# Keys, queries and values placed separately in the load order of an attention + MLP kernel, with a new list of nudges and the last stores in halves

## Chip, cores and metric

One core of one Trainium2 chip. The metric is the device time of that core in microseconds (us), lower is better.

## The reference

```python
def _attn_ref(q, k, v):                       # each (8, 8, 576, 64) fp32
    window = 128
    scores = scale * np.matmul(q, k.transpose(0, 1, 3, 2))
    bias = slopes[:, None, None] * (-np.abs(rel))[None, :, :]
    mask = (rel >= 0) & (rel < window)
    scores = np.where(mask, scores + bias[None], -1000000000.0)
    attn = softmax(scores)                    # cut
    return np.matmul(attn, v)

x = attn_out.transpose(0, 2, 1, 3).reshape(4608, 512)
h = x @ w_in                                  # 512 -> 2048
r = np.maximum(h, 0.0)
return (r * r) @ w_out                        # 2048 -> 512
```

A query looks at itself and the 127 rows before it, so a block of 128 queries needs two blocks of keys. The MLP needs all heads of a row, so a group of 512 rows of `x` can start once its four blocks of attention are done.

## The kernel before

The kernel builds a list of tasks (a load, a burst of matmuls, an exponential, ...) with dependencies, ring buffers, durations and a priority key. A planner in Python works through them with these assumed durations and fixes one order for each engine. On the chip every engine then works in its order, waiting for whatever is late. So keys, slacks and the list of nudges `ADJ` change only orders, never the work.

```python
FIRST = ["b0", "b1", "b2", "b3", "i0", "i1", "i2", "o0", "i3", "i4", "o1", "o2", "b4", "o3", "b5", "b6", "b7"]
N_PE = 8
SLACK = {"kq": 0.0, "kqT": 5000.0, "v": 4000.0, "x": 2000.0}
FILL = 0.7
LEAD = 480
SIZE = {"kq": 4, "v": 9, "kqT": 7, "P": 3, "x": 6}
```

`b` is a block (first 128 rows of one batch) with its keys, queries and values, `i` a piece of `w_in`, `o` a piece of `w_out`. All of these are cast from fp32 to bf16 by DMAs issued on GpSimd, in the planned order; only k0 and q0 come over other queues.

```python
    def load_block(m, key):
        # ... cut: block 0 comes unconverted over the other queues
            def fetch_kq():
                for i, src in enumerate((k, q)):
                    nc.gpsimd.dma_start(view(kq[s_kq[m].idx], i), source(src, m, split))
        # ...
        def fetch_v():
            nc.gpsimd.dma_start(tile_of(s_v[m])[0:n, :, 0:D], source(v, m))
        l_v = plan.add({"POOL": 890.0}, key + 0.2, fetch_v, ...)

    for i, what in enumerate(FIRST):
        n = int(what[1:])
        key = EARLY + 100 * (i + 1)
        if what[0] == "b":
            load_block(n, key)
        else:
            load_w("in" if what[0] == "i" else "out", n, key)
```

Blocks 0 to 7 are transposed on TensorE (`tp` for keys and queries, `xp` for the attention's output), blocks 8 to 39 by DMA transposes on SyncE's queue (`kqT<-kq`, `xT<-x`), which also issues the stores, all in one order.

```python
        if m >= N_PE:
            def flip_x():
                nc.sync.dma_start_transpose(out=xT[:, :, t0:t0 + n], in_=xt[sx.idx][0:n, :])
            t_x[m] = [plan.add({"SP": 1200.0}, due, flip_x, t_n, [], [sx], dma=900.0 * n / 128, name=f"x{m}",
                               slack=SLACK["x"])] * 2
            return
```

Where the planner sees a hole in TensorE's work it places "fillers", useless matmuls on a tile of zeros:

```python
    def fill(task, slot):
        for _ in range(int(task.gap * FILL / 56.0) if task.gap > 200.0 else 0):
            nc.tensor.matmul(slot.tile[:, 0:128], warm[:, 0:128], warm[:, 0:128], start=True, stop=True)
```

Names below: `s` are scores, `P` their exponentials, `pv` the products with the values, `h` the first MLP product, `rt` its relu, `g` the square, `o` the second product. "Group 3" is the fourth group of 512 rows, the first whose four blocks (13 to 16) are all transposed by DMA and used in one go.

The softmax here doesn't subtract the row's maximum and nothing guards it: scores larger than these inputs give would overflow.

## Time and profile before

| | before |
|---|---|
| median of 3 executions | 313.81 us (313.56 to 314.08) |
| span of the profiled one | 311.8 us |
| TensorE starts useful work | 4.58 us |
| lost on TensorE from 4.58 to 25 us | 7.30 us |
| lost on TensorE from 25 us to its end | 8.63 us |
| TensorE ends | 308.78 us |
| tail after it | 3.00 us |

"Lost" is elapsed time less the useful matmuls at their unhindered start-to-start price. The prediction has 7.5 and 8.3 for the two losses; the figures here come from counting useful weight loads (each matmul has one). The profiled execution, at 313.56 us, was the fastest of the three. The prediction shows the lines behind this table. These are three lines of the timelines of ScalarE and TensorE of the kernel before (start, length, engine, line, operation, out<-in, shapes, count, and the idle time before it with what ended it):

```profile
18.73 1.51 ACT L337 ACTIVATE masks<-dist 128x128 bf16<-128x128 f32 x7
20.15 1.05 ACT L762 ACTIVATE rt<-h 128x512 bf16<-128x512 f32 x2
20.77 2.84 PE L798 MATMUL h<-xT,w_in_sb 128*128 128x128 bf16 x48 [0.41 <-ACT rt L762]
```

TensorE stops until 20.77 for a bank of `h`, because the relu that frees the bank stands on ScalarE behind seven mask tiles that nobody needs yet.

### The profile page before, as it was taken

To read this page: it belongs to the slowest core of one execution; us is meant where nothing else is said; L and a number is where in the kernel's file an instruction comes from. 1 tells how busy PE (TensorE), PEld (TensorE's weight loads), DVE (VectorE), ACT (ScalarE), POOL (GpSimd) and SP (SyncE) were. 2 spreads that over 40 slices of the span, in tenths; PEclk is the share of its full clock that TensorE was granted. 3 is DMA by queue.
4 is the path that set the end of the run, shared out by engine and by line. 5 is a ranking of instruction groups with operands and counts; after the bars stand their busy time and mean duration, and the time that the engine had idled before them with its cause. 6 is when DMAs were issued, how large, how long until landed. Compare 5 with 4: busy or idle time off the path is not lost.

```text
span 311.8 us, 7044 instructions
## 1 busy us (share of the span) xinstructions
PE 304.3 (98%) x2767; PEld 173.3 (56%) x2767; DVE 165.5 (53%) x493; ACT 170.9 (55%) x327; POOL 106.4 (34%) x132
## 2 busy tenths in 40 slices
PE   7789999999999999999999999999999999999996
PEld 3588757774676664455555455555444444444443
DVE  5574275675586776687577657776222222222211
ACT  3785456493476376876678737764443444444400
POOL 8953595386622828206747091000000000000000
PEclk9999999999999999999999999999999999999999
DMA  9999999999999999969999999612011100010022
GB/s 129 167 205 206 173 196 176 151 207 161 187 189 176 155 154 203 173 83 139 157 200 182 160 178 151 159 35 69 34 36 57 44 36 35 35 34 36 34 96 72
DMA packets 166242, 39.52 MB, mean 127 GB/s; under 512 B 156353, under 2 KB 161729, under 8 KB 166209
## 3 DMA queue, kind: packets, MB, share of 16 engines
q0 software_dynamic: 115184, 18.10, 83.7%
q1 hardware_dynamic: 50592, 20.65, 33.1%
q8 instruction: 21, 0.34, 0.4%
q10 hardware_dynamic: 432, 0.33, 0.4%
q14 instruction: 13, 0.10, 0.1%
HBM read 36.70 MB, written 9.44 MB: 148 GB/s over the span
## 4 chain that ended last, share of the span: by engine, by line
PE 95%; ACT 2%; DVE 1%; issue 0%; ACTq 0%
PE o L842 40%; PE h L815 27%; PE h L798 13%; PE pv L668 6%; PE s L564 5%; PE wm L475 1%; PE tp L505 1%; ACT P L633 1%; PE s L616 1%; ACT masks L337 1%; ACT kqf L299 1%; PE xp L714 0%; DVE kqf L297 0%; PE s L625 0%; ACT rt L762 0%
## 5 line engine op out<-in xcount | busy, mean ns | idle before, releaser
L842 PE MATMUL o<-w_out_sb,g 128*128 128x512 bf16 (+2 forms) x592 | 142.6, 373 | 0.0
L762 ACT ACTIVATE rt<-h 128x512 bf16<-128x512 f32 (+1 forms) x145 | 86.1, 602 | 95.0 <-PE h L815 70.2
L771 DVE TENSOR_TENSOR g<-rt 128x512 bf16<-128x512 bf16 (+1 forms) x145 | 60.8, 420 | 100.5 <-ACT rt L762 99.4
L815 PE MATMUL h<-xT,w_in_sb 128*128 128x512 bf16 x384 | 97.1, 379 | 0.0
L842 PEld LDWEIGHTS <-g 128*128 128x128 bf16 x592 | 54.1, 98 | 57.0
L588 ACT ACTIVATE P<-s 128x512 bf16<-128x512 f32 x120 | 62.1, 609 | 8.0 <-PE s L564 8.0
L815 PEld LDWEIGHTS <-w_in_sb 128*128 128x128 bf16 x384 | 35.5, 98 | 40.1
L448 POOL DMA_DIRECT2D kq<-in_k_dram x39 | 33.7, 863 | 43.6 <-DMA kqT<-kq 38.0
L798 PE MATMUL h<-xT,w_in_sb 128*128 128x128 bf16 (+1 forms) x512 | 46.0, 246 | 0.4 <-ACT rt L762 0.4
L596 DVE TENSOR_TENSOR P<-P,masks 128x512 bf16<-128x512 bf16 x96 | 39.1, 418 | 8.5 <-ACT P L588 5.3
L798 PEld LDWEIGHTS <-w_in_sb 128*128 128x128 bf16 x512 | 39.0, 98 | 5.5 <-issue 0.5
L453 POOL DMA_DIRECT2D vt<-in_v_dram x32 | 27.3, 854 | 27.9 <-PE pv L668 27.5
L448 POOL DMA_DIRECT2D kq<-in_q_dram x39 | 33.8, 866 | 6.0 <-DMA w_out_sb<-in_moe_w_out_dram 1.8
L694 DVE TENSOR_TENSOR x<-pv,rec 128x256 bf16<-128x256 f32 (+1 forms) x80 | 32.1, 417 | 0.9
L668 PEld LDWEIGHTS <-P 128*128 128x128 bf16 (+1 forms) x576 | 24.2, 101 | 11.9 <-DVE x L694 1.3
L299 ACT ACTIVATE osb<-o 128x512 f32<-128x512 f32 (+1 forms) x23 | 13.4, 583 | 21.2 <-PE o L842 21.2
L668 PE MATMUL pv<-vt,P 128*128 128x65 bf16 (+1 forms) x448 | 22.9, 194 | 0.0
L297 DVE COPY osb<-o 128x512 f32<-128x512 f32 (+1 forms) x14 | 9.5, 681 | 14.7 <-PE o L842 14.4
L564 PEld LDWEIGHTS <-kqT 64*128 64x128 bf16 x448 | 12.4, 94 | 7.6 <-issue 7.0
L685 DVE RECIPROCAL rec<-pv 128x4 f32<-128x4 f32 (+1 forms) x80 | 12.6, 171 | 6.7 <-PE pv L668 5.7
L564 PE MATMUL s<-kqT 64*128 64x128 bf16 (+1 forms) x256 | 15.6, 210 | 0.0
L564 PE MATMUL s<-kqT,kqT 64*128 64x128 bf16 (+1 forms) x192 | 11.4, 210 | 0.0
(45 smaller groups left out, 100.5 us busy)
## 6 DMA issues: line engine op xcount, KB each, us to landing
out_dram<-osb SPq DMA_DIRECT2D x31, 256.0 KB, 5.0
kq<-in_k_dram POOLq DMA_DIRECT2D x31, 128.0 KB, 6.5
kq<-in_q_dram POOLq DMA_DIRECT2D x31, 128.0 KB, 6.8
vt<-in_v_dram POOLq DMA_DIRECT2D x24, 128.0 KB, 6.8
w_out_sb<-in_moe_w_out_dram POOLq DMA_DIRECT2D x4, 512.0 KB, 15.2
w_in_sb<-in_moe_w_in_dram POOLq DMA_DIRECT2D x3, 512.0 KB, 11.5
vf<-in_v_dram POOLq DMA_DIRECT2D x8, 128.0 KB, 6.3
out_dram<-osb SPq DMA_DIRECT2D x8, 128.0 KB, 2.4
```

The source lines that it names most:

```text
L448: nc.gpsimd.dma_start(view(kq[s_kq[m].idx], i), source(src, m, split))
L453: nc.gpsimd.dma_start(tile_of(s_v[m])[0:n, :, 0:D], source(v, m))
L564: nc.tensor.matmul(sS[2 * g2 + r].tile[:, jj * 256 + c0:jj * 256 + c0 + w], tile_of(s_kqT[mk])[rows, c, :], tile_of(s_kqT[mq])[rows, C + c ...
L588: nc.scalar.activation(flat(Pt[sP.idx]), sS[i].tile.rearrange("p (j t) -> p j t", j=2)[:, :, lo:hi], AF.Exp, bias=0.0, scale=scale)
L596: nc.vector.tensor_tensor(flat(Pt[sP.idx]), flat(Pt[sP.idx]), flat(masks), op=ALU.mult)
L668: nc.tensor.matmul(sv.tile[0:n, hi * (D + 1):(hi + 1) * (D + 1)], prob, tile_of(s_v[mk])[:, h, 0:D + 1], start=mk == parts[0][1], stop=mk ...
L694: nc.vector.tensor_tensor(o, heads(sv)[0:n, :, 0:D], sr.tile[0:n, :].unsqueeze(2).to_broadcast([n, 4, D]), op=ALU.mult)
L762: nc.scalar.activation(srt.tile[:, 0:n], slot.tile[:, 0:n], AF.Relu, bias=0.0, scale=1.0)
L771: nc.vector.tensor_tensor(o, i, i, op=ALU.mult)
L798: nc.tensor.matmul(slot.tile[:, f * w:(f + 1) * w], w_in_sb[:, cc, fc * 128:(fc + 1) * 128], xT[:, cc, lo:lo + w], start=cc == 0, stop=cc ...
L815: nc.tensor.matmul(slot.tile, w_in_sb[:, cc, fc * 128:(fc + 1) * 128], xT[:, cc, g * 512:(g + 1) * 512], start=cc == 0, stop=cc == C - 1)
L842: nc.tensor.matmul(slot.tile[:, 0:hi - lo], gt[:, fc, t * 128:(t + 1) * 128], w_out_sb[:, fc, lo:hi], start=fc == 0, stop=fc == FCB - 1)
```

## The change

Its intent: new orders found by replaying the plan with random late landings. Keys/queries (`k`) and values (`v`) of a block get places of their own in the load order; the first piece of `w_in` comes third; the first piece of `w_out` comes before the third of `w_in`; blocks 4 to 7 come last. The last stores before the final one go out in halves. Slacks, the lead of attention, the planner's tie-breaking and all nudges are new.

```diff
-FIRST = ["b0", "b1", "b2", "b3", "i0", "i1", "i2", "o0", "i3", "i4", "o1", "o2", "b4", "o3", "b5", "b6", "b7"]
+FIRST = ["k0", "k1", "i0", "v0", "v1", "k2", "v2", "k3", "v3", "i1", "o0", "i2", "i3", "i4", "o1", "o2", "o3", "k4", "k5", "v4", "k6", "k7", "v5", "v6", "v7"]
+N_XP = 8
+HALVED = [(7, 1), (7, 2), (7, 3)]
-SLACK = {"kq": 0.0, "kqT": 5000.0, "v": 4000.0, "x": 2000.0}
+SLACK = {"kq": 0.0, "kqT": 4500.0, "v": 2000.0, "x": 2500.0}
-LEAD = 480
+LEAD = 1200
 ADJ = {
-    "e12.3": -99552.96, "e17.1": 266.08, ...          # cut: 64 nudges out
+    "b3": 8899994.7, "e13.1": 299208.63, ...          # cut: 59 others in
-    NEAR = {"PE": 60, "ACT": 120, "DVE": 60}
+    NEAR = {"PE": 25, "ACT": 250, "DVE": 0}
-                for t in c:
+                for t in c[:8] if e == "POOL" else c:
-    def load_block(m, key):
+    def load_block(m, key, v_key=None):
-        l_v = plan.add({"POOL": 890.0}, key + 0.2, fetch_v, ...
+        l_v = plan.add({"POOL": 890.0}, key + 0.2 if v_key is None else v_key, fetch_v, ...
-        if m >= N_PE:
+        if m >= N_XP:
         def store():
-            for i, (b, kb) in enumerate(ranges[4 * g + t]):
+            rows = [(b * S + kb * 128, i * 64, blk[kb]) for i, (b, kb) in enumerate(ranges[4 * g + t])]
+            if (g, t) in HALVED:
+                rows = [(r + 64 * i, 64 * i, 64) for r, _, _ in rows for i in range(2)]
```

Cut: the staging buffer of block 0 becomes a ring with one user, and candidates are kept sorted by key. Line numbers after the change are 8 higher in most of the body.

## The prediction

> **What bounds the kernel now.** I read the page first, then busy time by stretches, then the groups of TensorE by shape, the chain of waits over the first 25 us, the timeline of the start and the landing times of the loads. The page says TensorE, nearly alone:
>
> ```profile
> PE 304.3 (98%) x2767; PEld 173.3 (56%) x2767; DVE 165.5 (53%) x493; ACT 170.9 (55%) x327; POOL 106.4 (34%) x132
> PE   7789999999999999999999999999999999999996
> PE 95%; ACT 2%; DVE 1%; issue 0%; ACTq 0%
> ```
>
> Only the first three slices (7.8 us each) and the last are not full. Busy time over four stretches (start, middle, pure MLP, tail):
>
> ```profile
> 4.58:25.00 20.42, 17.09 (x236) 13.16 (x235) 12.34 (x55) 13.19 (x37) 15.18 (x19) 1.00 1.74 185
> 25.00:216.00 191.00, 191.00 (x2082) 116.14 (x2081) 128.03 (x376) 120.98 (x228) 87.40 (x105) 1.00 1.66 162
> 216.00:308.78 92.78, 92.78 (x446) 42.87 (x444) 22.16 (x50) 34.63 (x58) 0.00 (x0) 1.00 0.13 45
> 308.78:311.80 3.02, 0.00 (x1) 0.00 (x0) 0.00 (x0) 0.28 (x1) 0.00 (x0) 1.00 0.25 87
> ```
>
> Columns: length, then busy us (instructions) of PE, weight loads, DVE, ACT, POOL, then clock, DMA share, GB/s. From 25 us until 308.78 TensorE never idles. But a busy PE need not be at its peak, so I took the start-to-start times of the matmuls. In the pure MLP stretch a matmul of 512 columns starts every 216 ns, which is 512 columns at 2.4 per ns plus 2.5 ns; groups of eight of 128 columns come 55.8 ns apart. Pricing every matmul so (two of 64 rows side by side count as one) gives this account of the 311.8 us:
> - 0 to 4.58: warm-up, first load and cast. 4.58 is the first useful matmul.
> - 288.3 us of useful matmuls.
> - 8.3 us lost between 25 and 308.78. Of that 6.4 us are the 30 bursts of 64-row score matmuls, which cost about 119 ns on leaving and 95 ns on entering (30 x 0.214); the rest is mostly the switches to and from pv, 7 to 20 ns each. No stall over 150 ns.
> - 7.5 us lost between 4.58 and 25 (3.3 idle, 0.9 filler matmuls on the zero tile, the rest pipe gaps); useful work done by 16 us is only 5.35, by 22 us 10.0.
> - 3.0 us tail after the last matmul.
>
> So a different order can win only in the start (7.5 us) and a little in the tail. The start hangs on loads. The timeline of GpSimd shows them issued early, then waiting:
>
> ```profile
> 1.34 1.03 POOL L453 DMA_DIRECT2D vf<-in_v_dram  x1 [0.16 <-issue]
> 2.36 0.89 POOL L448 DMA_DIRECT2D kq<-in_k_dram  x1
> ...
> 10.37 2.29 POOL L394 DMA_DIRECT2D w_in_sb<-in_moe_w_in_dram  x3
> 12.58 0.82 POOL L397 DMA_DIRECT2D w_out_sb<-in_moe_w_out_dram  x1
> ...
> 20.00 0.87 POOL L453 DMA_DIRECT2D vf<-in_v_dram  x1 [1.66 <-DMA w_in_sb<-in_moe_w_in_dram]
> 22.52 0.75 POOL L397 DMA_DIRECT2D w_out_sb<-in_moe_w_out_dram  x1 [1.65 <-DMA w_out_sb<-in_moe_w_out_dram]
> ```
>
> The landings in the trace come one after another, in the order of issue: v0 6.24, k1 7.08, q1 7.92, v1 8.77, k2 9.64, q2 10.48, v2 11.32, k3 12.16, q3 13.08, v3 13.88, i0 15.18, i1 16.52, i2 19.70, o0 22.23, i3 24.78, i4 27.36, o1 29.87, o2 32.41, q4 34.15, v4 34.98, o3 37.73, q5 39.48, v5 40.30, and so on to v7 46.85 (k, q, v: block numbers; i, o: pieces of w_in and w_out). A block tile costs 0.85 us of this stream, a 256 KB weight piece 1.3, a 512 KB piece 2.55. The queue is one saturated pipe up to about 45 us. TensorE's stalls in the start sit between these landings:
>
> ```profile
> L625 PE MATMUL s<-kqf 64*128 64x128 bf16 x32 | 2.2, 218 | 1.3 <-DVE kqf L297 0.9
> L668 PE MATMUL pv<-vf,P 128*128 128x65 bf16 x32 | 1.9, 193 | 0.7 <-ACT P L633 0.7
> L278 PE MATMUL tp<-warm 128*128 128x128 bf16 x12 | 0.9, 222 | 0.0
> ```
>
> They are named after the evacuation and the exponential, the links of one block's chain; they show because no other block and no MLP work is there to fill them. The MLP's first matmul starts at 16.01, one us after i0.
>
> **What the Trainium skill says.** "DMA: Bandwidth & Descriptors", section "Issuing engines are not separate DMA queues": all issuers share the same 16 engines and interleave. The trace agrees: DMA is at 9 tenths in nearly every slice up to slice 26, so the order of the list, not the number of queues, decides when a piece lands. "TensorE: Matmul & The Clock Gate", section "Back-to-back issue gap", gives N/2.4 + 2.5 ns as the warm isolated gap and about 131 ns as the sustained figure at N=512. The trace has 216 ns in 220 back-to-back w_out matmuls, so the first form holds here and the second does not; there is no headroom in the MLP. "TensorEngine Tiling (Array Packing)", section "Key Properties": changing the tiling mode drains the engine; here 95 to 119 ns a switch, 6.4 us in all, and the change keeps the number of score bursts. "Perfetto Trace Analysis", section "Identifying the Most-Contended Engine", warns that matmul busy share is no measure of headroom; hence the account by start-to-start times.
>
> **The change part by part.**
> 1. *Load order.* New: k1 q1, i0, v0, v1, k2 q2, v2, k3 q3, v3, i1, o0, i2, i3, i4, o1, o2, o3, k4 q4, k5 q5, v4, k6 q6, k7 q7, v5, v6, v7. The same bytes, so v7 again lands near 46.9. With the durations above, from the same first landing (6.24): q1 7.1 (0.8 earlier), i0 8.4 (6.8 earlier), v0 9.25, v1 10.1, q2 11.8, v2 12.65, q3 14.35, v3 15.2 (1.3 later), i1 16.5 (same), o0 19.1 (3.1 earlier), i2 21.6 (1.9 later), i3 24.2, i4 26.7, o1 29.2, o2 31.8, o3 34.3 (3.4 earlier), q5 37.8, v4 38.6, v5 43 (2.7 later). v0 at 9.25 is no loss: the first exponentials end at 9.26.
>  Working TensorE through this: block 1's transposes and scores come some 1.2 us earlier; x0 is transposed near 11.3 and the first MLP unit (0.45 us) runs in a gap, since i0 is there. By 16.5 the four blocks (about 1.56 us of useful matmuls each, less the last block's pv and transpose) and that unit make about 6.25 us, against 5.7 before. From 16.5 on TensorE should not stall: 2.7 us of units, pv and transposes, 0.9 for the fourth block's unit, then at 19.1 two token tiles of o with the first w_out piece (2 x 0.86, limited by two o banks), which reaches 21.9, past i2 at 21.6. Useful by 21.9: 11.6 us, against 9.9 before. **Gain 1.7 us**, carried to the end because everything later is full. The filler matmuls cost nothing but what waiting would.
> 2. *After 25 us.* i2 to i4 bring 3.57 us of matmuls each per 2.55 us of stream, so no stall to 34; group 0's down projection lasts to about 44.7, and blocks 4 to 7 (keys earlier, v5 later) make about 5 us in between, just enough for v5 at 43. Gain or loss 0.
> 3. *LEAD 480 to 1200*, slacks v 4.0 to 2.0, kqT 5.0 to 4.5, x 2.0 to 2.5, other tie-breaking, a new list of nudges. Attention of blocks 8 to 39 is asked for earlier. It cannot remove work; TensorE was full anyway: 0. It moves attention's end, now at 214 us (last pv), to the left by perhaps 10 us, and GpSimd's idle stretch of 130 to 140 us should shrink.
> 4. *Halved stores.* (7,1) to (7,3) are single 128-row tiles, so three more store DMAs between about 265 and 290 us, where the store queue is idle: no cost. They shift the completion semaphores by three: 109 such DMAs, the last on lane 5 of 8, become 112, the last on lane 8. In the trace the last landing is at 310.69, the queue then steps through the three semaphores behind it at 60 ns each. That goes: **0.18 us**.
> 5. N_XP equals N_PE, the stage ring has one user: 0.
>
> Sum: 313.81 - 1.7 - 0.18 = 311.9.
>
> **Rivals.** (a) *The start gains nothing*: blocks 2 and 3 land up to 1.3 us later, and i2, the piece that ended the shortage before, 1.9 us later; if the o tiles do not fill 19.1 to 21.6 (their squares are late, or the o banks are taken), TensorE waits for i2 and the gain is given back: 313.5 to 315. For it: the filling margin is only 0.3 us. Against it: the plan was searched over replays. (b) *A wait returns in the middle*: smaller slack on v and earlier attention put in-order TensorE behind late loads, with 6.5 us from issue to landing in the busy phase and the transposes taking 5.5. Every stall lengthens the kernel: 314 to 317. Against it: the stated aim is to bear late landings. (c) *The start gains more*: 7.5 us are lost there and only about 1 us is mode switches; if k1 first also closes the chain gaps of 7.5 to 12 us, 3 us go: 310.5.
>
> **Range and chances.** Repeats differ by 0.5 us. The centre is the sum; rival (c) sets the low end at 309.8, rival (a) and a mild (b) the high end at 313.9. Over 2% faster would be below 307.5, that is 6.3 of the 7.7 us that can be had at all: 3%. Slower than 320.1 needs stalls of 6 us in a middle that has none: 2%.
>
> **What would show it.** i0 landing near 8.4 and a first MLP matmul near 11.5; k1's scores near 8.3 instead of 9.5; o matmuls before those with i2; useful matmuls by 22 us about 11.6; TensorE full from 16.5; the lost time after 25 us again near 8.3; 30 bursts; three more stores and a tail of 2.8. It is wrong if TensorE idles at 19 to 22 us or 40 to 50 us, or if stalls over 150 ns appear after 25 us.

## The result

| | before | after |
|---|---|---|
| median of 4 executions each, same rounds | 313.94 us (313.56 to 314.10) | 313.51 us (312.99 to 313.73) |
| ratio after/before | | 0.9986, interval 0.9968 to 1.0003 |

A ratio here is the mean time of one kernel's fast runs over the mean of the other's fast runs of the same rounds, so it is not quite the ratio of the medians quoted. The change came out at about -0.4 us where -1.9 was predicted; the time is inside the range, and "within 2%" holds. The interval includes 1, so these four executions alone do not show a gain.

The page of the kernel after (busy share of the engines, TensorE's 40 slices, and the chain that ended last):

```profile
PE 302.0 (97%) x2748; PEld 174.1 (56%) x2792; DVE 166.0 (53%) x496; ACT 169.4 (54%) x324; POOL 106.2 (34%) x132
PE   8899999999999999999999999999999999999996
PE 93%; DVE 2%; DMA 1%; issue 1%; ACT 1%; SPq 0%; DVEq 0%
```

The first three slices now read 8, 8, 9 instead of 7, 7, 8: a small step in the start and nothing elsewhere. A trap: 2748 matmuls against 2767 does not mean less work. 44 matmul records are missing in this trace (2792 weight loads); the weight loads, which are complete, give the same 2744 useful ones in both kernels. The new plan also has 40 fillers where the old one had 15, so "busy" rose in the start by more than the useful work.

Busy time by stretches after (length, then busy us and instructions of PE, weight loads, DVE, ACT, POOL, then clock, DMA share, GB/s):

```profile
4.58:25.00 20.42, 18.51 (x268) 14.42 (x270) 12.41 (x53) 12.70 (x38) 15.02 (x19) 1.00 1.74 182
25.00:216.00 191.00, 188.20 (x2037) 115.82 (x2067) 127.77 (x379) 120.59 (x226) 87.39 (x105) 1.00 1.70 161
216.00:308.30 92.30, 91.88 (x442) 42.69 (x448) 22.82 (x53) 34.04 (x57) 0.00 (x0) 1.00 0.16 46
308.30:311.10 2.80, 0.00 (x1) 0.00 (x0) 0.00 (x0) 0.28 (x1) 0.00 (x0) 1.00 0.27 94
```

PE shows 18.51 busy in the start against 17.09 before, 1.4 us more; of useful work there is only 0.56 us more (13.68 by 25 us against 13.12), most of the rest are fillers. In the middle PE shows 188.20 of 191, but the missing records are there: the weight loads run through without a stall. The account of the two profiled executions:

| part | before | after | gain |
|---|---|---|---|
| lost 4.58 to 25 us | 7.30 | 6.74 | 0.56 |
| lost from 25 us to TensorE's end | 8.63 | 8.71 | -0.08 |
| tail | 3.00 | 2.83 | 0.17 |
| span | 311.78 | 311.14 | 0.65 |

(The stretches above and in the prediction end at 311.1 and 311.8, so they read 2.80 and 3.02 for the tails.) So the tail gave what was predicted, the middle gave its nothing, and the start gave a third. The tail is 3.00 and 3.02 us in the two profiles of the kernel before, and 2.82 to 2.84 in all others, e2 and e8 among them, which add the halved stores to the kernel before. The start before, on TensorE:

```profile
10.61 0.41 PE L668 MATMUL pv<-vf,P 128*128 128x65 bf16 x8
16.01 0.61 PE L798 MATMUL h<-xT,w_in_sb 128*128 128x128 bf16 x8
17.38 0.40 PE L714 MATMUL xp<-ident,x 128*128 128x128 bf16 x4 [0.39 <-DVE x L694]
```

and after:

```profile
9.59 0.28 PE L676 MATMUL pv<-vf,P 128*128 128x65 bf16 x4
13.52 0.61 PE L806 MATMUL h<-xT,w_in_sb 128*128 128x128 bf16 x8
17.36 0.40 PE L722 MATMUL xp<-ident,x 128*128 128x128 bf16 x4 [0.21 <-DVE x L702]
20.07 1.03 PE L850 MATMUL o<-w_out_sb,g 128*128 128x512 bf16 x3
22.02 4.18 PE L806 MATMUL h<-xT,w_in_sb 128*128 128x128 bf16 x72
```

The first MLP unit runs at 13.52 (predicted 11.5). Block 2's output is transposed at 17.36, and from there TensorE has no stall. The hole of before at 20.4 is gone: `o` matmuls stand at 20.07, since the first piece of `w_out` landed at 19.72 instead of 22.23. All of the start's gain arises from here on (whether by the load or by the new order of ScalarE, no run separates). Up to 17.3 us both kernels have done exactly the same set of useful matmuls: everything that the new order brings before that, it loses before that too.

Landings after, with the predicted ones in brackets: q1 7.19 (7.1), i0 8.60 (8.4), v0 9.45 (9.25), v3 15.93 (15.2), i1 17.21 (16.5), o0 19.72 (19.1), i2 22.32 (21.6), o3 35.35 (34.3), v4 39.63 (38.6), v7 47.08 (46.9).

### The profile page after: what moved, and what is told of

It is laid out like the page before. It is cut to its first block, busy times and chain, and to the rows that moved or that the text cites. A ratio compares the mean times of both kernels' runs of the same rounds, so it can differ in the third digit from the quotient of the medians.

```text
span 311.1 us, 7054 instructions
## 1 busy us (share of the span) xinstructions
PE 302.0 (97%) x2748; PEld 174.1 (56%) x2792; DVE 166.0 (53%) x496; ACT 169.4 (54%) x324; POOL 106.2 (34%) x132
## 4 chain that ended last, share of the span: by engine, by line
PE 93%; DVE 2%; DMA 1%; issue 1%; ACT 1%; SPq 0%; DVEq 0%
PE o L850 40%; PE h L823 27%; PE h L806 14%; PE pv L676 6%; PE s L572 5%; DMA stage<-in_q_dram 1%; PE tp L513 1%; DVE x L702 1%; PE xp L722 1%; PE s L633 0%; ACT kqf L306 0%; ACT P L641 0%; DVE kqf L304 0%; DVE kq L304 0%; SPq L438 0%
## 5 line engine op out<-in xcount | busy, mean ns | idle before, releaser
L850 PE MATMUL o<-w_out_sb,g 128*128 128x512 bf16 (+2 forms) x564 | 137.7, 373 | 2.3 <-issue 1.1
L823 PE MATMUL h<-xT,w_in_sb 128*128 128x512 bf16 x370 | 94.8, 379 | 0.8 <-issue 0.3
L604 DVE TENSOR_TENSOR P<-P,masks 128x512 bf16<-128x512 bf16 x96 | 38.6, 418 | 11.6 <-ACT P L596 9.1
L676 PEld LDWEIGHTS <-P 128*128 128x128 bf16 (+1 forms) x576 | 24.2, 101 | 11.5 <-DVE g L779 1.3
L304 DVE COPY osb<-o 128x512 f32<-128x512 f32 (+1 forms) x19 | 13.0, 685 | 17.2 <-PE o L850 13.0
L306 ACT ACTIVATE osb<-o 128x512 f32<-128x512 f32 (+1 forms) x18 | 10.4, 580 | 21.5 <-PE o L850 21.5
```

What stands on the lines that cost most here:

```text
L604: nc.vector.tensor_tensor(flat(Pt[sP.idx]), flat(Pt[sP.idx]), flat(masks), op=ALU.mult)
L676: nc.tensor.matmul(sv.tile[0:n, hi * (D + 1):(hi + 1) * (D + 1)], prob, tile_of(s_v[mk])[:, h, 0:D + 1], start=mk == parts[0][1], stop=mk ...
L823: nc.tensor.matmul(slot.tile, w_in_sb[:, cc, fc * 128:(fc + 1) * 128], xT[:, cc, g * 512:(g + 1) * 512], start=cc == 0, stop=cc == C - 1)
L850: nc.tensor.matmul(slot.tile[:, 0:hi - lo], gt[:, fc, t * 128:(t + 1) * 128], w_out_sb[:, fc, lo:hi], start=fc == 0, stop=fc == FCB - 1)
```

## The experiments

The profile after leaves these questions: is 0.65 us typical; what ate the start's gain; and does the middle always stay full? All variants gave the reference's result. The variants of orders use this after the planner has run:

```python
    by = {t.name: t for t in done}
    def put(name, ahead_of):                  # move one task in the order of emission
        t = by[name]
        done.remove(t)
        done.insert(done.index(by[ahead_of]), t)
```

| run | kernel | mean us | before, same rounds | ratio (interval) |
|---|---|---|---|---|
| e1 | after, unaltered | 314.02 | 314.07 | 0.9999 (0.9966 to 1.0032) |
| e2 | before + relu ahead + halves | 314.23 | 314.07 | 1.0005 (0.9992 to 1.0019) |
| e3 | after, fillers merged | 314.50 | 314.07 | 1.0009 (0.9992 to 1.0026) |
| e4 | after's orders, old loads | 316.10 | 314.07 | 1.0065 (1.0052 to 1.0078) |
| e5 | before, one look | 313.77 | | |
| e6 | after, one look | 313.48 | | |
| e7 | after + `x` transposes first | 313.30 | 314.14 | 0.9972 (0.9957 to 0.9987) |
| e8 | e2 + new late loads | 315.24 | 314.14 | 1.0034 (1.0020 to 1.0049) |
| e9 | e7, i0 late | 313.72 | 314.14 | 0.9986 (0.9974 to 0.9999) |
| e10 | e7 + other banks | 313.17 | 314.14 | 0.9969 (0.9956 to 0.9981) |
| e11 | e7, no fillers | 313.41 | 314.14 | 0.9979 (0.9965 to 0.9993) |
| e12 | e7, v0 before i0 | 312.91 | 314.04 | 0.9963 (0.9951 to 0.9975) |
| e13 | e10 and e12 together | 312.92 | 314.04 | 0.9964 (0.9952 to 0.9977) |

The letters in the expectations name theories; each is put in words below where it is judged.

### e1: the kernel after once more

No edit.

> The changed kernel unaltered, as a control beside the others. Both theories: 0.4 to 0.5 us faster than the kernel before (ratio 0.9985), span of the profiled run 311 to 312 us. If a second profile again shows 3 TensorE stalls between 11.7 and 17.4 us, w_in piece 1 landing near 17.2 and a 16 KB instruction fetch packet near 13.7 us, these are properties of the program and not of one run.

Measured: 317.1, 313.31, 313.49, 313.14, 313.23 and 313.85 us. Five runs lie 0.66 us under before's mean of 314.07; one is 3.7 above them, and that is the one that was profiled. TensorE around 117 us, in the first profile after:

```profile
117.15 5.13 PE L823 MATMUL h<-xT,w_in_sb 128*128 128x512 bf16 x23
```

and in this one:

```profile
119.67 4.65 PE L823 MATMUL h<-xT,w_in_sb 128*128 128x512 bf16 x13 [2.07 <-issue]
```

TensorE idles 2.07 us ahead of the first `w_in` matmul of group 3. The page says "issue", so one has to look for the missing input: the `x` transposes of blocks 13 to 16. SyncE's queue in the first profile after:

```profile
91.66 10.86 SPq L499 DMA_TRANSPOSE kqT<-kq  x4
103.24 5.50 SPq L709 DMA_TRANSPOSE xT<-x  x4
```

and in this one:

```profile
91.94 14.69 SPq L499 DMA_TRANSPOSE kqT<-kq  x4
107.36 6.52 SPq L709 DMA_TRANSPOSE xT<-x  x4
```

The four key/query transposes (blocks 17 to 20) ahead wait for loads that came late here (q19 landed at 101.4 and q20 at 105.3; 96.7 and 100.6 in the first profile after), and everything behind them on the in-order queue waits too. The last `x` transpose lands at 119.6 instead of 116.4. In the first profile after the margin (from that landing to the matmul that needs it) was 0.71 us; in the first of before it was 4.06, its last one landing at 113.2. There the same four key/query transposes stand ahead of three of the `x` transposes; that of block 13 goes before them, with block 12's:

```profile
94.98 5.41 SPq L491 DMA_TRANSPOSE kqT<-kq  x4
105.23 3.79 SPq L701 DMA_TRANSPOSE xT<-x  x3
```

A second loss follows, in the windows of this run:

```profile
117.00:119.70 2.70, 0.63 (x11) 0.42 (x10) 1.86 (x7) 0.15 (x1) 0.00 (x0) 1.00 1.77 159
119.70:124.00 4.30, 4.30 (x13) 1.59 (x14) 0.77 (x2) 1.19 (x2) 0.82 (x1) 0.60 1.69 181
```

The granted clock is 0.60 in the second stretch: eight matmuls of 512 columns start 427 to 430 ns apart instead of 216, which is 1.7 us more. Against the first profile after, 2.2 us are lost at the wait, 1.7 at the halved clock and 0.3 earlier (v0 and the fourth piece of `w_in`, i3, landed later), 4.2 in all, the difference of the spans. So the prediction's rival (b), a wait that returns in the middle, is real, but in some executions only.

### e2: the removed hole alone, in the kernel before

```diff
+HALVED = [(7, 1), (7, 2), (7, 3)]            # and the store of the change
+    put("reluu0.1.0", "mask0.4")             # relu of the second unit ahead of four masks
```

> The kernel before with its old load order and its old order on TensorE; only one ScalarE instruction (the relu of the second MLP unit) goes ahead of four of the mask exponentials, and the three stores are halved. Theory R (the new load order earns nothing; the gain is the TensorE gap of 0.57 us at 20.4 us, which ends when ScalarE has done its masks, plus 0.18 us in the tail): faster than the kernel before by 0.5 to 0.75 us, as fast as the changed kernel or faster; the gap at 20.4 us is under 0.1 us. Theory L (the load order earns the gain): at most 0.2 us faster, since the tail alone is left.

Measured: 313.32 to 314.77 us, mean 314.23 against 314.07: no gain. In its profile (313.32 us, span 311.5) the hole at 20.4 is gone; TensorE runs through it:

```profile
19.27 3.90 PE L799 MATMUL h<-xT,w_in_sb 128*128 128x128 bf16 x63
```

At this point TensorE is 0.61 us ahead of before. 0.22 of it is given back at 21.66, and the rest by 45.6, where the transposes of block 7 wait 0.30 us for q7, which lands at 45.6 (44.7 in before's profile). TensorE ends 0.06 us earlier; the rest of the span's gain is the tail. So in this execution the gain of the start did not last. q7 landed 0.9 later than in before's profile (45.0 in e5); at 44.7 TensorE would not have waited for it. Whether scatter or the edit made it late stays open, and so does why four of the six runs, none of them profiled, took 314.5 to 314.8. A gain in the start is "carried to the end because everything later is full" only if no later load comes late.

### e3: fillers merged, to move the instruction fetch

The landings from v3 on were 0.7 us later than predicted. In the trace a 16,384-byte instruction packet of TensorE runs from 13.7 to 14.7 us, just ahead of v3 (q3 lands at 14.57); with 25 more fillers it comes 3 us earlier than in before (16.8). Here four fillers become one matmul of 512 columns, 54 rows fewer in TensorE's program.

```diff
-        for _ in range(int(task.gap * FILL / 56.0) if task.gap > 200.0 else 0):
-            nc.tensor.matmul(slot.tile[:, 0:128], warm[:, 0:128], warm[:, 0:128], start=True, stop=True)
+        left = int(task.gap * FILL / 56.0) if task.gap > 200.0 else 0
+        while left:
+            w = 4 if left >= 4 else 1
+            nc.tensor.matmul(slot.tile[:, 0:128 * w], warm[:, 0:128], warm[:, 0:128 * w], start=True, stop=True)
+            left -= w
```

> The changed kernel with its 40 filler matmuls of 128 columns merged into pieces of 512 columns: the same filler time with some 54 fewer TensorE rows early on. Theory F (TensorE's own instruction fetch[...] falls 3 us earlier because of the fillers and holds back v of block 3 and w_in piece 1 by 0.6 us): the first fetch packet moves from 13.7 to after 16 us, v3 lands near 15.4 instead of 15.9 and w_in piece 1 near 16.6 instead of 17.2. The time then improves by 0.6 us if the landing of w_in piece 1 was what kept TensorE from filling up at 16.5, and by less than 0.2 us if the chain of evacuations of block 2 (last TensorE wait ends at 17.36 on a VectorE result) sets it. Rival: fetches do not matter and the landings stay.

Measured: 313.29 to 315.33 us. The fetch moved from 13.7 to 17.2 us and v3 lands 0.84 us after q3 instead of 1.36, so the fetch explains most of the late v3 (theory F). It is not so in every profile: in e10 the fetch starts at 14.74, and v3 lands 0.84 after q3 all the same. But TensorE's times did not move: block 2's `x` is transposed at 17.60, which is 7.80 after the first `pv`, the same 7.80 as in the first profile after. The late weight piece was not the limit.

This profile (of the 315.28 us run) has the stall of e1 again, here named. From the waits after 25 us (engine, tile, line, what for: us in total, times, longest):

```profile
PE h L826 <- DMA xT<-x: 2.0, 1, 2.0
```

After this wait the matmuls start 216 ns apart: the clock was not halved. So of four profiles with this order of SyncE's queue and the new loads (the first of the kernel after, e1, this one, and e6 below) two show the stall. The runs at 314.90 and 315.33 look like it too, but were not profiled.

### e4: the new engine orders with the old order of loads

```diff
+    LOADS = ['lv0', 'lkq1', 'lv1', 'lkq2', 'lv2', 'lkq3', 'lv3', 'w_in0', 'w_in1', 'w_in2', 'w_out0', 'w_in3', 'w_in4', 'w_out1', 'w_out2']
+    for name in LOADS:
+        done.remove(by[name])
+    i = done.index(by["iota"]) + 1
+    done[i:i] = [by[name] for name in LOADS]
```

> The changed kernel with the order of the first 15 loads of the kernel before; the instruction orders of all other engines are those of the change. In-order TensorE then waits for w_in piece 0 until about 15.2 us instead of 8.6 (its matmuls stand at 13.5) and for w_out piece 0 until 22.2 instead of 19.7 (its matmuls stand at 20.1). Theory L: 2.5 to 4 us slower than the changed kernel, since the order of TensorE needs these loads. Theory R says the same of this mix: it holds that the pair of load order and engine order moves together and that its net worth is nothing. A loss under 1 us would say that the loads are not on the path at all.

Measured: 315.48 to 316.61 us, 2.0 over before. TensorE reaches the first MLP unit at 13.4 and stands there until 16.05:

```profile
PE h L806 <- DMA w_in_sb<-in_moe_w_in_dram: 2.3, 1, 2.3
```

The clock is halved after that wait as well. Against e1 the loss is 2.1 us, or 2.7 without e1's slow execution (2.5 to 4 expected). The orders and the loads belong together; neither half can be priced alone.

### e5 and e6: before and after, one more look each

No edits.

> The kernel before, unaltered, profiled a second time. The margin between the landing of the x transposes of token group 3 and the first w_in matmul that reads them (4.06 us in the first profile) should again be over 1 us, and TensorE should again have one gap of 0.5 to 0.6 us at 20.4 us and none over 0.3 us after it. If it shows a gap at 117 us too, thin margins are not what the change added.

Measured: 313.77 us, span 312.0. The margin of group 3 is 1.86 us here (4.06 in the first profile), and there is a stall of 0.2 us at 82.7, where half of group 2 starts. e2's profile, with the same order of SyncE's queue, has a margin of 1.12 us. So the kernel before is thin in the middle too: 4.06, 1.86 and 1.12 us in three profiles, against 0.71, 1.02 and two stalls with the order of the kernel after.

> The changed kernel, unaltered, profiled a third time. Theory M (the change made a thin margin): the x transposes of token group 3 land within 1.5 us of, or after, the moment TensorE reaches them at 117.1 us; between 0 and 3 us are lost there, varying with the run. If the margin is 4 us as in the kernel before, the 2.5 us stall of the second profile was chance.

Measured: 313.48 us, span 311.7; margin 1.02, no stall. This run is 0.57 us longer than the first profile after, and the whole difference arises at one place:

```profile
10.16 0.28 PE L676 MATMUL pv<-vf,P 128*128 128x65 bf16 x4 [0.84 <-ACT P L641]
```

The first `pv` starts 0.57 later than the 9.59 above, and everything after stays shifted by about that, to the end. The bracket names the exponential, but the first of the block starts at 8.53 in this run and takes some 0.6 us, so it had long been done: v0 landed at 10.03. This is a wait for several semaphores put down to the wrong one.

### e7: the `x` transposes ahead of two key transposes

```diff
+    put("kqT19", "kqT21")
+    put("kqT20", "kqT21")                    # SyncE: both now behind x13 to x16
```

> The changed kernel with two key/query transposes (blocks 19 and 20) moved behind the four x transposes of blocks 13 to 16 in the SP queue; all else in its order. Theory M with its cause (the SP queue is in order, and the x transposes stand behind key/query transposes that wait for late loads): x of block 16 lands near 112 instead of 116 to 120, the margin at 117 us becomes 3 to 6 us, no run has the stall there, and all runs lie between 313.0 and 313.9 us; mean 0.3 to 0.9 us below the kernel before. Rival (the DMA engines, not the queue's order, delay the x transposes): the landings stay within 1.5 us of 116 and single runs still reach 315 us or more.

Measured: 312.95 to 313.50 us, mean 313.30 against 314.14. SyncE's queue:

```profile
92.04 6.24 SPq L499 DMA_TRANSPOSE kqT<-kq  x2
99.75 6.08 SPq L709 DMA_TRANSPOSE xT<-x  x4
```

The last `x` transpose of group 3 lands at 110.9; the margin is 6.58 us (5.80 to 7.70 in e9 to e13), and none of the 32 runs with this edit (e7, e9 to e13) is above 313.83. The theory that the thin margin makes the slow executions (theory M) stands, and this version beats the kernel before: interval 0.9957 to 0.9987. It was not run beside the kernel after; its mean of 313.30 is near the 313.40 of e1's five runs without the stall, so what it gains is the slow executions. Its profile differs from the first one after only by v0:

```profile
9.97 0.28 PE L676 MATMUL pv<-vf,P 128*128 128x65 bf16 x4 [0.49 <-DMA vf<-in_v_dram]
```

Here the right releaser is named. The profile ends TensorE 0.38 later, as much as v0 was later (9.83 against 9.45).

### e8: e2 with the late part of the new load order

```diff
+    LOADS = "w_out3 lkq4 lkq5 lv4 lkq6 lkq7 lv5 lv6 lv7".split()   # placed where lkq4 stood, on top of e2
```

> The kernel before with the one relu ahead of the masks, the halved stores, and of the new load order only its late part (third w_out piece, then k and q of blocks 4 and 5, v4, k and q of 6 and 7, v5 to v7). Theory S (TensorE cannot keep an early gain in the old order because q of block 7 lands at 44.7 us, just when TensorE reaches its transposes at 45.6): the 0.61 us won at 20.4 us are still there at 48 us, the transposes at 45.6 us do not wait; the profiled span is 0.6 to 0.8 us under that of the kernel before. Rival: the wait only moves to v of block 4 or 5, which lands later in the new order, and the gain is lost again by 50 us.

Measured: 314.94 to 315.65 us, worse. The old order of TensorE comes to block 4 at 34.9, and k4 now lands only at 36.1:

```profile
36.14 0.40 PE L506 MATMUL tp<-ident,kq 128*128 128x128 bf16 x4 [1.23 <-DMA kq<-in_k_dram]
36.97 0.40 PE L506 MATMUL tp<-ident,kq 128*128 128x128 bf16 x4 [0.43 <-DMA kq<-in_q_dram]
```

At these two waits (1.66 us idle) TensorE falls 2.0 us behind e2's profile; it ends 1.69 us later than in before's. The run was meant to show whether e2's gain survives with keys in the new places; the new waits cover that, so theory S stays undecided. It repeats e4's lesson from the other side.

### e9: w_in piece 0 back behind v3

```diff
+    for name in ("u0.0.0", "reluu0.0.0", "squ0.0.0"):
+        put(name, name.replace("0.0.0", "0.1.0"))
+    LOADS = "lkq1 lv0 lv1 lkq2 lv2 lkq3 lv3 w_in0 w_in1".split()   # on top of e7
```

> The kernel of the run with the x transposes first, with w_in piece 0 loaded after v of block 3 again (as in the kernel before; k and q of block 1 stay first), and the first MLP unit moved from 13.5 us to just ahead of the second unit. Theory N (loading w_in piece 0 early is worth nothing: its 0.45 us of matmuls come early, but k, q and v of blocks 2 and 3 come 1.3 us later): the weight loads after 20 us fall within 0.25 us of the run with the x transposes first, time within 0.3 us of it. Theory L (early w_in piece 0 earns the unit's time): 0.4 to 0.6 us slower.

Measured: mean 313.72, TensorE's end 0.43 later than in e7, as theory L said. That it is so near to the unit's 0.45 is partly luck. v0 landed at 8.22 here (9.83 in e7), so e9 was 0.25 ahead at block 2's `x` transpose; from there to the first `o` matmul it lost 0.68: 0.45 for the unit, which no longer fits in a hole, and 0.23 because a matmul of `h` had to wait at 18.4 for the `xT` just copied. Blocks 2 and 3 landed 1.6 us or more before those of e7 and brought nothing: from the first `pv` to block 2's `x` transpose it took 7.79 us again (theory N fell). So these loads do not set that chain's pace.

### e10: the `x` transposes of blocks 1 and 2 in other banks

```diff
             so = Slot(XP if m else "o")
+                if m in (1, 2):
+                    so.tag = "o"              # on top of e7
```

> The kernel of the run with the x transposes first; the x transposes of blocks 1 and 2 write the two PSUM banks that the down projection leaves unused until 20 us, instead of the two banks that they share with the key/query transposes and MLP units. Theory B (between 12.6 and 17.4 us TensorE waits on the two shared banks, not on loads: the second transpose of block 2 at 13.22 ends a wait on the ScalarE evacuation of the first): that transpose starts near 12.85, the x transpose of block 2 near 17.0 instead of 17.36, and 0.2 to 0.4 us are kept to the end. Rival (loads or VectorE set the pace there): under 0.1 us.

Measured: mean 313.17. From the first `pv` to block 2's `x` transpose it is now 7.42 us instead of 7.80 (both from weight load to weight load): sharing two banks between `pv`, `xp` and `tp` costs 0.38 in this chain. In the profile v0 came late (10.07) and hid 0.24 of it; i3, landing at 25.89, took the rest: TensorE's end is within 0.03 us of e7's. The means (313.17 and 313.30) differ by less than their intervals.

### e11: no fillers

```diff
-FILL = 0.7
+FILL = 0.0                                   # on top of e7
```

> The kernel of the run with the x transposes first, without its 40 filler matmuls (80 TensorE rows fewer in the first 17 us). If fillers stand in front of real work (4 of them, 0.22 us, run just ahead of the first transpose of block 2 at 11.93): 0.1 to 0.3 us faster. If they keep TensorE's clock up: matmuls after the idle stretches start-to-start at 107 ns for 128 columns in place of 56, 0.5 us or more slower. The first instruction fetch packet of TensorE should fall after 17 us, w_in piece 1 should land near 16.7.

Measured: mean 313.41. No clock drop and no gain: fillers neither help nor hurt here. The fetch falls at 17.3, v3 lands 0.83 after q3, i1 at 16.82, and again block 2's `x` transpose is 7.80 after the first `pv`.

### e12: v0 and v1 ahead of w_in piece 0

In all seven profiles with the load order of the change unaltered (after, e1, e3, e6, e7, e10, e11) the first `pv`, counted from its weight load, starts 0.10 to 0.11 us after v0's landing, which ranges from 9.45 to 10.07. (The expectation says eight; seven is right, since in e9 v0 lands at 8.22 and the exponential ends last.) The first exponential ends at 9.15 to 9.31 in these seven, so v0 is on the path.

```diff
+    LOADS = 'lkq1 lv0 lv1 w_in0'.split()      # on top of e7
```

> The kernel of the run with the x transposes first, with v of blocks 0 and 1 loaded ahead of w_in piece 0 (k and q of block 1 stay first; everything after as in the change). Theory V (the first pv matmul starts 0.10 us after v0 has landed, in all eight profiles of the new load order, and the x transpose of block 2 follows exactly 7.80 us later, so the landing of v0, 9.45 to 10.07 us, moves the whole kernel): v0 lands near 8.2, the first pv starts near 9.4 at the end of the first exponential, the x transpose of block 2 at 17.2; 0.3 to 0.6 us faster than the run with the x transposes first, span near 311.1 in every run, and the runs within 0.4 us of each other. Rival (v0 is only beside the path, and w_in piece 1 at 17.2 us sets the time): under 0.15 us.

Measured: 312.73 to 313.17 us, mean 312.91 against 314.04: -1.14 us, with e13 the lowest mean, and the runs lie within 0.44 us.

```profile
9.37 0.29 PE L676 MATMUL pv<-vf,P 128*128 128x65 bf16 x4
17.16 0.40 PE L722 MATMUL xp<-ident,x 128*128 128x128 bf16 x4 [0.21 <-DVE x L702]
20.17 1.02 PE L850 MATMUL o<-w_out_sb,g 128*128 128x512 bf16 x3
```

v0 lands at 8.37, a us before it is needed; the first `pv` now follows the exponential (end 9.27). Against e7's profile TensorE is 0.57 us ahead at the first `pv`, but only 0.28 after 20.17: there it meets the first piece of `w_out`, which landed at 20.13. The stream of loads is the next limit.

### e13: e10 and e12 together

```diff
+                if m in (1, 2):
+                    so.tag = "o"
+    LOADS = 'lkq1 lv0 lv1 w_in0'.split()      # on top of e7
```

> The same with the x transposes of blocks 1 and 2 in the two unused PSUM banks. In the run that tried these banks alone the x transpose of block 2 came 7.42 us after the first pv instead of 7.80, which a late v0 hid. Theory B: x transpose of block 2 near 16.85; the second MLP unit then waits for w_in piece 1 (17.0 to 17.6), so 0.1 to 0.3 us more than the run without the banks. Rival: w_in piece 1 takes all of it, difference under 0.1 us.

Measured: mean 312.92, no more than e12. Block 2's `x` transpose comes 7.41 after the first `pv` (17.02), so the bank edit works. The rival named the right kind of limit, not the right piece: in this profile TensorE is still 0.25 ahead of e12's at the first `o` matmul (the first `w_out` piece landed 0.25 earlier too), and loses 0.44 between 25 and 38 us, where i3, the third piece of `w_out` (33.73) and q4 (37.51) land later than in e12's.

## Why the prediction was wrong

**The step that failed is the "Gain 1.7 us" of the load order.** It measured 0.56 us in the first profile and less in most others: the first profile after had the earliest v0 of the seven, and e6's otherwise equal run was 0.57 us longer. Two sentences carried the error. Of the 1.14 us that the first profile lacks, v0 made about 0.2 (the first `pv` at 9.59, at 9.37 in e12), and the chain of the second sentence the rest (an estimate from these figures).

- "v0 at 9.25 is no loss: the first exponentials end at 9.26." The sum was nearly right (the exponential ended at 9.27), the reading was not. v0 landed at 9.45 to 10.07, always on the path, and up to block 2's `x` transpose each tenth that it was late was kept. A margin of 0.01 us on a stream whose landings scatter by 0.6 is a loss. e12 undoes this one place and moves the ratio from 0.9972 to 0.9963, with intervals that overlap; the profiles show the mechanism, v0 a us early and `pv` on the exponential instead.
- "From 16.5 on TensorE should not stall", with 6.25 us of useful work by then. It was 5.96 by 16.5, and TensorE was full only from 17.35 in the best profile. The four blocks' chain was taken to be limited by loads. Already block 1's scores came only 0.50 us earlier (9.03, before 9.53), not 1.2, though q1 landed as predicted. From the first `pv` to block 2's `x` transpose it took 7.78 to 7.80 us in eight profiles, e9 with much earlier loads among them; 0.38 of it are the shared banks (e10). The chain that the profile after gives for these 7.8 us is VectorE for half of it (3.9 us, 2.45 of them the normalisation `x`), ScalarE for 1.8 and TensorE for 1.75, and no load. That is inferred from semaphores; no run made VectorE's part shorter. So the predicted 11.6 us of useful work by 22 were 10.66. The first MLP unit at 13.52 instead of 11.5 stands in the same order, so it goes with this error (not tested apart).

**The table of landings** was right to 0.2 us up to v0 and 0.6 to 1.1 late from v3 to v4 (v7 again 0.2). 0.5 of that is the instruction fetch, by e3, brought forward by 25 more fillers ("the filler matmuls cost nothing but what waiting would" missed it). e3 and e11 show that it moves landings and not the end.

**Right in the start:** i0 early is worth about its 0.45 us (e9), and with o0 before i2 TensorE waits for no load after 17.4 us in the first profile after.

**The middle,** "gain or loss 0" and LEAD "0", held in the profile after (8.71 lost against 8.63), but it is a mean over executions that matters. One of eleven timed runs of the kernel after was at 317.1 because the landings used up the margin of group 3; e7 shows that it is the order of SyncE's queue. The change had moved one more `x` transpose behind the four waiting ones, though the order before was at times nearly as thin (4.06 to 1.12 us). Rival (b) named this mechanism, with a wrong place: late loads did hold up a queue, SyncE's and not TensorE's. That attention's end would move left by some 10 us failed without consequence: the scores of the last pair of blocks start at 210.4 us, 209.3 before. A build of the kernel after with LEAD alone put back (not run) has the same order of TensorE for about the first half of its instructions, and of SyncE's transposes to beyond group 3, so LEAD did not make that margin.

**Right:** the tail, 0.18 predicted and 0.17 measured. The wait that the last landing ends was followed by three more steps of some 60 ns; now it is the last one, since the last store is on the last of the eight semaphores.

**The chances:** rival (a) was the nearest, a start that gains little, but not for its reason: `o` matmuls did fill the time to i2 (20.07 to 22.02). The low end of the range, 309.8, is laid on rival (c), whose own sum is 310.5; nothing came near either.

Still open: why loads land up to 0.6 us later in one execution than in another of the same order, which part of the 7.80 us chain could be shortened, and what makes most runs of e2 slower than its profile.

## What to carry to other kernels

When a load is moved back until it lands "just as it is needed", count its scatter over executions as cost: look at the same landing in several profiles before calling it hidden. In a planned kernel, a load order and the engines' orders are one thing; changing one alone lost 1.1 to 2.0 us here. On an in-order queue, put the transposes that TensorE needs next ahead of those whose inputs may be late; two tasks moved gave a margin of 5.8 to 7.7 us, and none of 32 executions was slow.

## What the Trainium skill lacked or had wrong

- "TensorE: Matmul & The Clock Gate", section "Back-to-back issue gap": it gives about 131 ns per matmul as sustained at N=512; the runs show 216 ns, its isolated figure, in long back-to-back rows.
- The same page, section "What's actually happening": it ties the throttled clock to an idle window of about 3.4 us. Here 2.07 us without a matmul were followed by eight matmuls at 427 to 430 ns (e1), while 1.97 us were not (e3). The lengths are too near to each other to give a rule; but a wait well under the page's window was followed by a halved clock, in e4 too (2.3 us).
- "Runtime: NRT & Kernel Launch", section "Instruction fetch mechanics": blocks of 16 KiB per 256 instructions agree with the trace (16,384-byte packets, on average 251 recorded TensorE instructions apart in before's), and the page calls the cost mostly hidden. It lacks that loads under way can land later for it: with a fetch just before, v3 landed 1.31 to 1.88 us after q3 in six profiles (0.84 in a seventh, e10), and 0.83 and 0.84 in e11 and e3 without.
- No page that bears on this has the scatter of landings between executions of one kernel: v0 9.45 to 10.07 us in seven profiles, the last `x` transpose of group 3 116.4 to 119.6 us.
- No page that bears on this has the cost of the last store's semaphore: each one behind it is another step of 60 ns at the end, 0.17 us between the two tails here.
- "TensorEngine Tiling (Array Packing)", section "Key Properties", gives no number for the drain on a change of tiling mode; the trace shows 95 to 119 ns.
